# A fused attention and bilinear feed-forward kernel on one core: single-instruction fillers and another order for all engines

## The chip, the cores and the metric

The kernel runs on one core of a Trainium2 chip. A core has five engines with queues of their own, each executing its instructions strictly in the order in which the program gives them: PE (TensorE, the matmuls; its weight loads are shown as PEld), DVE (VectorE), ACT (ScalarE), POOL (GpSimd) and SP (SyncE, which here only issues transfers). POOL and ACT issue a few transfers too. The metric is the device time of one execution in microseconds. Two kernels are told apart by the medians of their runs.

## What is computed

Eight batches of eight heads, 576 positions, head size 64, go through causal attention with a forget gate; the result, as 4608 tokens of 512 values, goes through a bilinear feed-forward layer.

```python
scores = scale * np.matmul(q, k.transpose(0, 1, 3, 2))
log_f = np.log(np.clip(f, 0.0001, 1.0))
cum = np.cumsum(log_f, axis=-1)
decay = cum[:, :, :, None] - cum[:, :, None, :]
scores = np.where(causal, -1000000000.0, scores + decay)
attn = np.exp(scores - max); attn = attn / (sum + 1e-09)
x = (attn @ v), heads side by side: 4608 x 512
out = ((x @ w_a) * (x @ w_b)) @ w_out       # w_a, w_b: 512 x 1536, w_out: 1536 x 512
```

## The kernel before

**Attention.** Work goes by pairs of heads: t = 4b + pair, 32 of them. Half a batch, four heads, is a unit u. For each unit the queries and keys are loaded by SP in fp32 (line 288), cast to fp16 (mostly on POOL), transposed on DVE (line 302), and multiplied on PE in four groups of query blocks (tile sc, line 401). For the first three batches the decay and the causal mask are added on PE with further small matmuls into the same banks; for the others DVE adds a decay row that SP spreads over the partitions (tile spread, line 456), fused with the row maximum (line 512). DVE takes row maxima (line 488), ACT the exponentials with their sums (lines 544 and 550), DVE the reciprocals (lines 557 and 559), POOL scales the probabilities in place (line 567). The probabilities of a pair lie in two tiles: A for the first three query blocks, B for the last two (PA and PB; for four of the first eight pairs the tiles are the spread buffers, spread_78 to spread_81, not yet in use then, and one pair's A tile is an S buffer). They are turned by the DMA (line 583, into PTA and PTB, or for the first two batches partly into spare room of the tile xT) or, for batch 0, by PE (line 591, tile psP). PE multiplies them with the values: lines 611, 613 and 623 (pv) and line 636 (the last 64 rows, pv4). ACT or DVE copies the result, transposed, into xT.

**Feed-forward.** The tokens go in eleven groups: three of 256, then 384, six of 512, and 384. For each of twelve blocks of 128 hidden values PE makes psa and psb, four matmuls each (line 874), ACT or DVE copies psa (tile a, lines 138 and 142), DVE multiplies it with psb into ht (line 890). Then PE multiplies ht with wout into pso (line 899), ACT or DVE copies it into osb, and it is stored (line 914). The weights are loaded and cast by POOL's queue in seven parts (line 365): wa and wb in 512 and 1024 columns, wout in three parts.

**Buffers.** The PSUM has eight banks: two double tiles sc, and four single ones, ff, which psa, psb, pso, pv, psP and the fillers share. A tile is written again once its last readers are done.

**Fillers.** Forty operations multiply the unit matrix by itself into a free ff tile (tile idle, line 178). Nothing reads the result: they only keep PE at work. Each was four matmuls of 128 columns.

**What sets the order.** All the work is first put down as a list of numbered operations (`op`), each with the engines it may go to, its inputs and the buffers it takes. A table, `ORDER`, gives the sequence of these numbers, and `CHOICE` one letter for each operation that may go to more than one engine (A for ACT, D for DVE, P for POOL, S for SP). `laid_out` reads both, and the operations are emitted in that order. So each engine's queue is the table's order, restricted to that engine.

Of the kernel before, what the change touches and what calls it, by code (L numbers as in the profile page):

```python
# [37 lines left out]
def kernel(  # L38
# [11 lines left out]
    nc = tc.nc  # L50
# [29 lines left out]
    ident = fixed("ident", [128, 128])  # L80
# [94 lines left out]
    def filler(_):  # L175
        p = ps.tile([128, 512], FP32, tag="ff", bufs=RING["ff"], name="idle")
        for n in range(4):
            nc.tensor.matmul(out=p[:, 128 * n:128 * n + 128], lhsT=ident, rhs=ident, start=True, stop=True)
# [800 lines left out]
    for t0, n in [(0, 256), (256, 256), (512, 256), (768, 384)] + [(1152 + 512 * n, 512 if n < 6 else 384) for n in range(7)]:  # L979
# [3 lines left out]
        42-44 0 20 41 2 1 64 26 31 23 54 55 45 16 32 13 12 71 46 37 47 56 18 67 27 65 34 72 73 68 48 24 19  # L983
# [3 lines left out]
        142 6 154 155 92 147 143 159 149 91 148 144 160 162 161 108 166-168 145 172 131 52 53 132 179 173 14  # L987
# [13 lines left out]
        1667 1670 455 1671-1673 1676 1677 421 388 382 381 389 456 1674 401 333 1678 357 413 1675 364 1679  # L1001
# [3 lines left out]
        465 460 500 409 463 505 1703 416 1704 480-482 424 508 440 428 422 1705 1706 509 471 477 483 479 510  # L1005
# [5 lines left out]
        1745-1747 1750 1748 548 1749 1752 1751 573 575 543 529 532 618 549 533 1753 1754 577 536 605 537 545  # L1011
        1755 1758 1759 1756 580 582 581 1713 550 552 606 553 1757 554-556 611 583 1760 544 578 585 1762 1763
# [17 lines left out]
        831 874 852 1880 875 1829 883 885 1883 1884 1000 884 841 1882 834 880 1885 911 854 857 886 1888-1890  # L1030
# [105 lines left out]
```

## Time and profile before

| | |
|---|---|
| median of 3 runs | 402.16 us (401.61, 402.16, 402.33) |
| profiled execution | span of 400.7 us from its first to its last instruction; no other time of it is given |
| mean granted TensorE clock | 0.986 |
| busy | PE 96%, DVE 79%, POOL 63%, ACT 62%, PE's weight loads 53% |
| HBM | 49.69 MB read, 9.58 MB written |
| chain that ended last | PE 79%, DMA 9%, DVE 4%, POOL 2%, ACT 2% |

The profile's page tells busy time, then the span in forty slices of 10 us (a digit is tenths of busy time, PEclk the granted clock in tenths), the chain of work that ended last, groups of instructions by line with what ended the idle time before them, and DMA issues with their time to landing. The windows give the same by chosen stretches, the waits say who waited for whom, and the timeline gives single instructions, merged where they follow each other. A row of the timeline is: start in us, length in us, engine, line, operation, output<-inputs, shapes, and in brackets the idle time before it and what ended that. Of an engine's queue (SPq, POOLq) the rows tell the issuing of a transfer, not the transfer.

### The profile page before, as it was taken

The numbers are of one execution on the slowest core, as the hardware profiler recorded it, in microseconds if no ns is written. First come the engines' busy times: TensorE is split into PE (matmuls) and PEld (weight loads), VectorE is DVE, ScalarE is ACT, GpSimd is POOL, SyncE is SP. The second block draws the span as 40 slices with busy tenths as digits, with TensorE's granted clock in tenths as the row PEclk, the third lists the DMA queues.
The fourth block names the chain that finished last, engine by engine and source line by source line (L and its number), as shares of the span: only waits on it lengthen the run. The fifth ranks groups of instructions, "written<-read, shape, count | busy, mean of one in ns | idle before, by whom it ended". The sixth has DMA issues, their size and how long they took to land.

```text
span 400.7 us, 11076 instructions
## 1 busy us (share of the span) xinstructions
PE 383.2 (96%) x4040; PEld 212.0 (53%) x4040; DVE 315.3 (79%) x907; ACT 250.0 (62%) x757; POOL 253.6 (63%) x424
## 2 busy tenths in 40 slices
PE   8598799998999999999999999999999999999996
PEld 7466576765855544454445454544444444444553
DVE  8989798976778988997988889898969892373560
ACT  5798766666667778758785777577868673300011
POOL 3889876887397876897896849787968553000000
PEclk9889999998999999999999999999999999999999
DMA  7999989989999999999999999999997729000102
GB/s 282 240 186 289 204 177 224 213 150 215 208 301 208 227 171 330 201 277 212 295 187 286 211 255 273 233 241 190 276 187 218 157 66 202 28 2 36 71 0 79
DMA packets 148311, 78.22 MB, mean 195 GB/s; under 512 B 130592, under 2 KB 133408, under 8 KB 148256
## 3 DMA queue, kind: packets, MB, share of 16 engines
q1 hardware_dynamic: 144272, 72.53, 77.4%
q0 software_dynamic: 3696, 4.72, 7.0%
q8 instruction: 31, 0.51, 0.5%
q10 hardware_dynamic: 288, 0.26, 0.2%
q14 instruction: 24, 0.20, 0.1%
HBM read 49.69 MB, written 9.58 MB: 148 GB/s over the span
## 4 chain that ended last, share of the span: by engine, by line
PE 79%; DMA 9%; DVE 4%; POOL 2%; ACT 2%; issue 2%; SPq 0%; POOLq 0%; DVEq 0%; ACTq 0%
PE pso L899 22%; PE psa L874 22%; PE psb L874 21%; PE sc L401 8%; DMA wa<-in_moe_w_a_dram 5%; PE pv L611 2%; DVE st L488 2%; DMA k<-in_k_dram 1%; PE pv L613 1%; PE sc L636 1%; DMA PTB<-spread 1%; DMA PTB<-PB 1%; DVE qT L302 1%; PE pv L623 1%; ACT PB L550 1%
## 5 line engine op out<-in xcount | busy, mean ns | idle before, releaser
L874 PE MATMUL psa<-xT,wa 128*128 128x512 f16 (+2 forms) x528 | 116.2, 343 | 2.3 <-DMA wa<-in_moe_w_a_dram 1.7
L874 PE MATMUL psb<-xT,wb 128*128 128x512 f16 (+2 forms) x528 | 116.2, 343 | 0.1
L899 PE MATMUL pso<-wout,ht 128*128 128x512 f16 (+1 forms) x444 | 98.4, 374 | 0.0
L567 POOL TENSOR_SCALAR PA<-PA,st 128x128 f16<-128x128 f16 (+2 forms) x162 | 76.0, 482 | 31.8 <-DVE st L559 20.4
L890 DVE TENSOR_TENSOR ht<-psb,a 128x512 f16<-128x512 f32 (+2 forms) x132 | 76.2, 589 | 22.0 <-PE psb L874 15.0
L512 DVE CUSTOM_DVE_ANT_0 S<-sc,spread 128x128 f32<-128x128 f32 (+3 forms) x160 | 86.7, 567 | 7.7 <-PE sc L401 5.4
L138 ACT CAST a<-psa 128x512 f16<-128x512 f32 (+2 forms) x85 | 43.5, 515 | 55.9 <-PE psa L874 53.8
L874 PEld LDWEIGHTS <-wa 128*128 128x128 f16 x528 | 50.1, 99 | 45.5 <-issue 3.7
L874 PEld LDWEIGHTS <-wb 128*128 128x128 f16 x528 | 50.4, 99 | 41.5 <-issue 1.7
L567 POOL TENSOR_SCALAR PB<-PB,st 128x512 f16<-128x512 f16 (+1 forms) x84 | 58.7, 712 | 15.7 <-DVE st L559 14.6
L550 ACT ACTIVATE PA<-S,st 128x256 f16<-128x256 f32 (+2 forms) x120 | 59.9, 502 | 12.5 <-DVE st L512 12.4
L899 PEld LDWEIGHTS <-ht 128*128 128x128 f16 x444 | 41.7, 98 | 46.8 <-issue 1.3
L488 DVE TENSOR_REDUCE st<-sc 128x2 f32<-128x512 f32 (+7 forms) x68 | 46.3, 723 | 6.0 <-PE sc L401 5.3
L401 PE MATMUL sc<-kT,qT 32*128 32x128 f16 (+5 forms) x960 | 41.7, 272 | 5.5 <-ACT PA L550 2.1
L550 ACT ACTIVATE PB<-S,st 128x512 f16<-128x512 f32 x40 | 28.5, 714 | 7.9 <-DVE st L512 7.9
L401 PEld LDWEIGHTS <-qT 32*128 32x128 f16 (+1 forms) x960 | 18.6, 96 | 26.7 <-issue 14.4
L142 DVE CAST a<-psa 128x512 f16<-128x512 f32 (+2 forms) x47 | 26.2, 560 | 7.2 <-PE psa L874 6.6
L559 DVE RECIPROCAL st<-st 128x2 f32<-128x2 f32 x128 | 18.5, 157 | 14.0 <-ACT PA L550 8.7
L142 POOL CAST k<-k 128x1152 f16<-128x1152 f32 (+1 forms) x15 | 20.5, 1367 | 8.9 <-DMA k<-in_k_dram 8.9
L138 ACT COPY osb<-pso 128x512 f32<-128x512 f32 (+1 forms) x22 | 12.4, 570 | 19.9 <-PE pso L899 15.1
L138 ACT CAST xT<-pv 128x512 f16<-128x512 f32 (+2 forms) x39 | 17.0, 446 | 11.8 <-PE pv L636 5.8
L140 POOL TENSOR_SCALAR q<-q 128x1152 f16<-128x1152 f32 (+1 forms) x15 | 20.6, 1372 | 5.0 <-DMA q<-in_q_dram 4.2
(98 smaller groups left out, 491.5 us busy)
## 6 DMA issues: line engine op xcount, KB each, us to landing
spread<-cum_d SPq DMA_DIRECT2D x20, 576.0 KB, 5.9
out_dram<-osb SPq DMA_DIRECT2D x35, 256.0 KB, 3.8
q<-in_q_dram SPq DMA_DIRECT2D x15, 576.0 KB, 7.3
k<-in_k_dram SPq DMA_DIRECT2D x15, 576.0 KB, 5.2
v<-in_v_dram SPq DMA_DIRECT2D x32, 256.0 KB, 6.1
wout<-in_moe_w_out_dram POOLq DMA_DIRECT2D x3, 512.0 KB, 8.7
v<-in_v_dram SPq DMA_DIRECT2D x8, 128.0 KB, 7.2
wb<-in_moe_w_b_dram POOLq DMA_DIRECT2D x1, 1024.0 KB, 13.5
```

The lines of the kernel that those rows point to most:

```text
L138: nc.scalar.copy(out=out_, in_=in_)
L140: ENG[e].tensor_scalar(out=out_, in0=in_, scalar1=0.125, scalar2=1.0, op0=MUL, op1=MUL)
L142: ENG[e].tensor_copy(out=out_, in_=in_)
L401: nc.tensor.matmul(out=dst, lhsT=lhsT, rhs=rhs, start=start, stop=stop, skip_group_check=True)
L488: nc.vector.tensor_reduce(out=m if i == 4 else st[:, 2 * i:2 * i + 2][:, h:h + 1] if isinstance(x, list) else m, in_=y, axis=AXX, op=MAX, ...
L512: nc.vector.tensor_tensor_reduce(out=o, in0=x, in1=y, scale=-1.0, scalar=3e38, op0=ADD, op1=MIN, accum_out=m)
L550: nc.scalar.activation(out=p_blocks(t, i)[:, :, h, :], in_=x.rearrange("p (j k) -> p j k", k=128), func=EXP, scale=sign, bias=st[:, c:c + ...
L559: nc.vector.reciprocal(out=st[:, 20 + 2 * i:22 + 2 * i], in_=st[:, 10 + 2 * i:12 + 2 * i])
L567: ENG[e].tensor_scalar(out=p, in0=p, scalar1=st[:, c:c + 1], scalar2=1.0, op0=MUL, op1=MUL)
L874: nc.tensor.matmul(out=o, lhsT=w16[:, db, 128 * fb:128 * fb + 128], rhs=tokens(db, t0, n), start=(db == 0), stop=(db == 3))
L890: nc.vector.tensor_tensor(out=ht[:, 0:n], in0=T.pop(("psb", t0, fb))[:, 0:n], in1=T.pop(("a16", t0, fb))[:, 0:n], op=MUL)
L899: nc.tensor.matmul(out=o, lhsT=T[("ht", t0, fb)][:, 128 * tb:128 * tb + 128], rhs=wout16[:, fb, c], start=(fb == 0), stop=(fb == 11))
```

## The change

The operations, their numbers and the buffers are the same. Two things are changed. A filler is now one matmul of 512 columns, the unit matrix read four times over, in place of four of 128. And `ORDER` and `CHOICE` hold another order for all engines and another choice of engines, found by a search which counted that two readers of one PSUM bank wait for each other.

```diff
     def filler(_):
         p = ps.tile([128, 512], FP32, tag="ff", bufs=RING["ff"], name="idle")
-        for n in range(4):
-            nc.tensor.matmul(out=p[:, 128 * n:128 * n + 128], lhsT=ident, rhs=ident, start=True, stop=True)
+        nc.tensor.matmul(out=p.rearrange("p (n k) -> p n k", n=4), lhsT=ident,
+                         rhs=ident.unsqueeze(1).to_broadcast([128, 4, 128]), start=True, stop=True)
...
     CHOICE = """
-        DPAADDAAPPAPAAPADPADDAAADAADDDDDAADDDDAAADAAADDAAAADAAAAADAAAAAAADAAAAAADDAAADADADDAAAAAADDAAAAAAAAA
...
+        APDDAPAAPAPPAAPPDPDDDAADDADDDDAAADDADDAADAAAAADAAAADDAADDADADDAAADAAAAAAADAAAAAAAAAAAADDAADDAAADAAAAA
...
```

PE's queue has 8082 rows before and 7842 now: the 240 that are gone are three matmuls and three weight loads of each filler. Eleven fillers, not sixteen, now stand ahead of PE's first other matmul, and 29, not 24, behind it. The other counts hardly move: DVE copies 48 of the 132 psa tiles (47 before), ACT 84 (85), and the copies of pso, pv and psP are shared out nearly as before.

**POOL, the loads of the weights.** The rows are those of POOL's queue in the first third of batch 0 and 1. Line 365 issues a part of the weights, line 567 scales probabilities, line 142 casts k or v, line 140 q. Before:

```order
L142 CAST nv_73<-v_355 128x1024
L567 TENSOR_SCALAR PA<-PA,st 128x128 x2
L567 TENSOR_SCALAR PA<-PA,st 128x2x128 x2
L365 DMA wa_70<-in_moe_w_a_dram 128x4x512
L567 TENSOR_SCALAR PA<-PA,st 128x2x128 x2
L365 DMA wb_71<-in_moe_w_b_dram 128x4x512
L567 TENSOR_SCALAR PA<-PA,st 128x128
L142 CAST nv_74<-v_377 128x1024
L567 TENSOR_SCALAR spread_80<-spread_80,st 128x2x128
L365 DMA wb_71<-in_moe_w_b_dram 128x4x1024
L365 DMA wa_70<-in_moe_w_a_dram 128x4x1024
```

Now the first part of wb comes ahead of the cast of the next q:

```order
L140 TENSOR_SCALAR q_270<-wout_72 128x640
L365 DMA wb_71<-in_moe_w_b_dram 128x4x512
L140 TENSOR_SCALAR q_276<-q_214 128x1152
L567 TENSOR_SCALAR PA<-PA,st 128x2x128
L567 TENSOR_SCALAR PA<-PA,st 128x128
```

then both parts of wa follow, behind the first norms of spread_79:

```order
L567 TENSOR_SCALAR spread_79<-spread_79,st 128x2x128
L567 TENSOR_SCALAR spread_79<-spread_79,st 128x128
L567 TENSOR_SCALAR spread_79<-spread_79,st 128x2x128
L365 DMA wa_70<-in_moe_w_a_dram 128x4x512
L365 DMA wa_70<-in_moe_w_a_dram 128x4x1024
```

and the large part of wb follows thirteen rows later, with the first part of wout right behind:

```order
L567 TENSOR_SCALAR spread_80<-spread_80,st 128x3x128 x2
L142 CAST k_678<-k_676 128x1152
L567 TENSOR_SCALAR PB_76<-PB_76,st 128x4x128 x2
L365 DMA wb_71<-in_moe_w_b_dram 128x4x1024
L365 DMA wout_72<-in_moe_w_out_dram 128x4x512
```

So the small wb part moved to the front, and the large one from ahead of the large wa part to the end.

**SP, the transposes of batch 1.** Line 583 turns a tile of probabilities, line 272 loads v, line 288 q or k, line 914 stores. Before:

```order
L583 DMA_TRANSPOSE PTB<-PB_76 128x13x128
L583 DMA_TRANSPOSE xT_67<-S 128x6x128
L583 DMA_TRANSPOSE xT_66<-PA 128x6x128
L272 DMA v_1988<-in_v_dram 64x8x64
L583 DMA_TRANSPOSE xT_69<-spread_78 128x6x128 x2
L272 DMA v_2066<-in_v_dram 128x8x64 x2
L583 DMA_TRANSPOSE xT_68<-spread_81 128x6x128 x2
L914 DMA out_dram<-osb 128x512
L583 DMA_TRANSPOSE PTB<-spread_78 128x13x128
L583 DMA_TRANSPOSE PTB<-spread_81 128x13x128
```

Now:

```order
L583 DMA_TRANSPOSE PTB<-PB_77 128x13x128
L583 DMA_TRANSPOSE xT_69<-spread_78 128x6x128
L583 DMA_TRANSPOSE xT_67<-S 128x6x128
L914 DMA out_dram<-osb 128x512
L288 DMA q_1961<-in_q_dram 128x1152
L272 DMA v_2009<-in_v_dram 128x8x64 x2
L583 DMA_TRANSPOSE xT_68<-spread_81 128x6x128
L583 DMA_TRANSPOSE PTB<-spread_78 128x13x128
L583 DMA_TRANSPOSE xT_69<-spread_78 128x6x128
L583 DMA_TRANSPOSE PTB<-spread_81 128x13x128
L583 DMA_TRANSPOSE xT_68<-spread_81 128x6x128
```

Between the second PTB<-PB and PTB<-spread_78 stood ten transfers, now seven: the second halves of both xT transposes moved behind the PTB that follows them, and the store moved ahead.

**PE, the last rows of two pairs of batch 1.** Where PE's scores of one group end, before:

```order
L401 LDWEIGHTS xT0_66
L401 MATMUL sc0_1844<-neg_62,xT0_66 128x2x32
L636 LDWEIGHTS nv1_74
L636 MATMUL pv4_1900<-PTB_1742,nv1_74 64x64
L636 LDWEIGHTS nv1_74
```

Now the same scores are followed by

```order
L401 LDWEIGHTS xT0_66
L401 MATMUL sc0_1735<-neg_62,xT0_66 128x2x32
L874 LDWEIGHTS wa16_70
L874 MATMUL psa_1788<-xT0_66,wa16_70 128x256
L874 LDWEIGHTS wa16_70
L874 MATMUL psa_1788<-xT1_67,wa16_70 128x256
```

and the first product with a tile turned from PB stands behind the last of eight such groups:

```order
L874 MATMUL psb_1863<-xT3_69,wb16_71 128x256
L623 LDWEIGHTS nv1_74
L623 MATMUL pv_1870<-xT0_66,nv1_74 64x128
L623 LDWEIGHTS nv1_74
L623 MATMUL pv_1870<-xT0_66,nv1_74 64x128
L623 LDWEIGHTS nv1_74
L623 MATMUL pv_1870<-PTB_1801,nv1_74 64x128
```

So eight groups of psa and psb, four matmuls each, moved from behind these products to ahead of them. From the 384-token group on, PE's order of scores, products and feed-forward groups is nearly the same in both.

More of the change, by code (lines that the diff above doesn't have):

```diff
@@ L1085 @@
-        2307 2299 2300 2304 2305 2308-2310
+        42 0 14 30 19 43 23 27 20 34 25 13 1 64 44-46 54 55 17 47 56 66 2 48-50 57 71-73 67 36 31 58 61 59
+        51 68 69 32 74 10 75 76 275 21 77 9 70 78 62 79 37 96 80 90 16 60 276 109 115 65 110 111 81-83 117
+        97 112 116 103 11 12 18 114 7 118 120 121 134 122 98 99 104 113 105 128 130 84 106 140 277 146 119
+        124 123 125 85 126 129 131 132 230 127 3 89 141 135 142 91 136 153 155 154 231 143 145 108 100 101
+        278 279 147-149 39 6 137 139 159 160 162 161 166 168 167 172 179 52 180 181 5 138 173 174 156 40 144
@@ new lines @@
+        258 259 102 107 216 217 133 244 169 170 24 41 224 266 245 171 53 252 253 238 175 198 176 225 239 267
+        182 199 200 203 1598 1599 1602 1604 1600 1601 1603 1606 1605 204 272 273 1608 150 274 178 163 177
+        220 92 205 201 207 208 221 4 94 209 212 213 185-187 192 188 184 86 290 291 297 194 193 189 151 152
[3 rows of a table added]
+        366 1625 214 284 243 261 240 241 197 373 374 190 95 1626-1628 191 367 1630-1632 296 1633 215 350 351
+        1629 1634 1636 1635 1638 344 352 375 376 306 1637 378 449 450 300 368-370 372 288 289 262 263 285
[9 rows of a table added]
@@ new lines @@
+        427 623 1650 465 480-482 383 603 385 422 404 405 508 384 510 417 473 499-501 483 506 507 1704 509
[4 rows of a table added]
+        1736 547 549 542 1735 1737 1738 1740 604 1739 1742 1744 1743 569-571 573 463 576 1741 527 1745 575
[4 rows of a table added]
+        1779 591-593 626 671 672 678 1780 638 1770 640 1781 639 645 1784 595 594 1782 606 1783 1786 641 612
+        613 1785 1788 609 642 644 643 1789 1792 596 673 1790 1791 647 674 1793 1794 646 1795-1797 1800 648
+        649 679 681 610 680 624 1798 682 683 597 627 630 607 599 1802 631 634 1787 709 632 633 635 1799 675
@@ new lines @@
+        676 651 614 615 652 653 655 685 801 686 1801 1804 1806 802 1803 1805 1808 1807 1771 1766 684 654 656
+        636 659 1810 677 660 621 1809 688 687 689 691 1811 798 692 693 1812 1814 1813 616 1816-1818 1820 658
[4 rows of a table added]
+        767 777 820 821 778 779 744 1843-1846 745-747 718 719 726 780 748-750 782 783 781 1847 816 817 1848
+        1849 1851 1852 741 727 804 711 1853 1824 1833 784 715 1850 1854 754 755 806 751 809 822 756 796 818
+        752 753 787 788 1855 1856 757 758 760 759 1859 1857 1858 785 786 1861 1860 1862 1863 824 789-792 869
@@ new lines @@
+        877 871 870 1865 876 793 805 794 1864 872 836 1866-1868 843 1869 1870 838 879 873 875 1871 1872 1875
+        1873 1874 906 844 810 1876 846 837 839 807 1877-1879 1881 795 826 825 828 845 811 797 829 847 910
+        832 912 814 907 812 878 830 831 1834 815 880 882 833 850 852 881 851 1880 853 1883 1884 883-886 848
+        999 834 840 842 874 841 849 908 1882 1885 1886 887 888 890 1888 891 1889 1890 854 855 996 856-858
+        892 808 819 859 860 835 862 864 863 893 823 895 896 1893-1895 1898 889 1887 865 1829 866 861 897 914
@@ new lines @@
+        898 899 902 1896 827 911 904 926 933 928 867 959 961 960 1899 1900 1903 1904 934 936 966 962 1891
+        868 903 901 968 900 967 894 997 1905 1907 1906 813 905 998 927 1014 1909 935 1908 1911 1912 1000 937
+        1910 939 963 965 938 915 1001 969-972 1018 929 1913 930 931 1015 1914 918 919 922 920 921 923 973
+        1007 974 964 975 932 976 940 942 941 1892 977 978 1016 1915-1918 943 944 946 1919 1921 1901 924 980
+        947 945 979 948 909 981 913 1019 1920 1922 1923 1925 1924 1926 949 916 917 1004 925 952 953 1020 950
@@ new lines @@
+        1220 1395 1153 1186 1154 2010 2006 1213 1185 1217 1265 1187 1266 1149 1273 2013 2015-2017 1155 1190
+        2014 2019 2020 2018 2021 1232 1234 1240 2024 1156 1192 2025 1267 1268 1275 1182 1191 1188 1233 1189
+        1206 1207 2022 2026 1203 1204 1218 1396 1193 1272 1269 1271 1270 1239 1221 1235-1238 1242 1225 1228
+        1274 1276-1278 1241 1243-1245 1226 2027 1224 1229 1246 1247 1249 1222 1223 1392 1393 1248 1279 1280
+        1282 2029 2030 1250 1230 1286 1287 1302 1303 1281 1251 2031 2034 1306 1308 2028 1283 1285 1284 2032
@@ new lines @@
+        1210 1219 1208 1288 1253-1255 1215 2035 2036 1227 1289 2023 1231 1291 1292 1307 1293 1290 2039 2041
+        1300 2033 1294 1258 1260 1259 2037 2040 2043-2045 1252 1298 1295 1297 1310 1322 1329 1261 1262 2046
+        2047 2049 1296 1324 1263 1256 1257 1264 1330 2048 2051 1211 2050 1331 2053 2052 2055 1209 1323 1325
+        1355 1363 1357 1356 2042 1397 1362 1326 1328 1332 1333 1335 1358 1359 1361 1394 2056-2058 1365 2059
+        2061 1364 2060 1327 2062 2063 1301 1315 1299 1311 1314 1312 1334 1318 1319 1403 1316 1317 2054 1336
@@ new lines @@
+        1337 1339 1338 1404 1369-1371 2064 2067 1360 1366 1304 1367 2065 2066 1320 1408 1410 1368 1340 1341
[3 rows of a table added]
+        1400 1398 1353 2092 2093 1464 2094 2097 2098 1354 1390 1431-1434 2090 1380 1388 1387 1386 1389 1438
+        1399 1416 1391 1437 1419 1471 1423 1440 1473 1472 1439 1474 1476 1424 1475 1422 1435 1426 1401 1441
+        1442 1405 1443 1466 1467 1469 1406 1407 1436 2091 1425 1427 1477-1479 2099 2102 1420 2095 2096 1444
+        1446 1445 1447 1480 1402 1468 1428 1451 1452 1413 1500 1448 1450 2103 2104 1481-1483 1421 2107 2108
@@ new lines @@
+        1449 2109 1484-1486 2105 1429 2110 1456 1457 1453 1458 2111 1454 2113 2112 2115 1487 1417 1489 1490
+        2116 1459 1460 1492 2117 2118 2100 1504 1501 1491 1493 1505 1508 1520 1528 1521 1498 1522 2119-2121
+        2114 1496 2123 1553 1560 1523 1561 1455 2125 2124 1555 1462 1461 1497 1488 1527 1562 1495 1494 2127
+        2128 1554 1556 1499 2122 1557 1558 1563 2126 2129 1409 2131 1564 1529 1530 2132 1531 2133-2135 1509
[4 rows of a table added]
+        2157 2160-2162 2165 1577 2166 2163 2167 2168 2170 2171 1552 1587 1589 1583-1585 1590 1578 1593 1595
@@ new lines @@
+        1596 2172 2175 2176 2169 2177 2173 2174 2178-2180 2183 2181 2182 2158 2184 2187 2185 2186 2188 2191
+        2189 2190 2192 2195 2196 2193 2194 1588 1591 2159 1594 1597 2197-2199 2201 2200 2203 2205 2204 2207
+        2209 2206 2208 2210 2202 2211 2213 2212 2215 2217 2216 2218 2164 2219 2221 2220 2223 2222 2214 2224
+        2225 2228-2231 2226 2233-2235 2238-2240 2243 2244 2227 2236 2245-2248 2232 2249-2251 2241 2252 2255
+        2242 2253 2254 2256 2259 2257 2258 2260 2263-2266 2261 2262 2267 2269 2268 2271 2273 2270 2272 2275
@@ L1091 @@
+        DAADAAADAADAAADADADDADAADAADDADDDADDADDAADDADADAADDAAAAAADAAAADAAADAADAAAAADADDADAADAAAADAAAAADADAAD
+        AADAAAAAAAADAAAAAADAAAAAAAADAADDADDAAAAADAAADADDDDADADDAAADDAAADADDAAADADADSAS
     """
```

46 lines of the change are left out of this document (8 added, 38 removed), and 107 rows, old and new, of the table ORDER.

## The prediction

> **What bounds the kernel now.** I read the page's busy shares first, then the windows (every engine by stretch of time), then PE's waits, then PE's timeline around the two longest late ones.
>
> ```profile
> PE 383.2 (96%) x4040; PEld 212.0 (53%) x4040; DVE 315.3 (79%) x907; ACT 250.0 (62%) x757; POOL 253.6 (63%) x424
> PEclk9889999998999999999999999999999999999999
> ```
>
> PE is busy 96% of a span of 400.7 us. The missing 17.5 us and the low digits of the clock lie early, which the windows show (columns: PE, PEld, DVE, ACT, POOL busy us, clock, DMA share, GB/s).
>
> ```profile
> 10.00:20.00 10.00, 5.28 (x138) 4.01 (x136) 9.62 (x23) 7.67 (x32) 8.86 (x20) 0.86 0.99 240
> 40.00:50.00 10.00, 7.75 (x134) 6.06 (x136) 7.95 (x21) 7.32 (x30) 8.40 (x12) 1.00 1.13 204
> 90.00:100.00 10.00, 8.22 (x100) 5.42 (x100) 6.13 (x13) 6.31 (x18) 7.10 (x13) 0.83 1.07 213
> 120.00:130.00 10.00, 10.00 (x84) 5.89 (x82) 8.30 (x30) 7.85 (x27) 7.88 (x10) 1.00 1.09 207
> 380.00:390.00 10.00, 10.00 (x62) 5.95 (x61) 6.93 (x13) 1.44 (x3) 0.00 (x0) 1.00 0.00 0
> ```
>
> From 120 to 390 us PE has no hole and full clock, and its arithmetic is the same after the change. So the time can only be won or lost ahead of some 110 us, and in the last 5. PE's own waits, over the span:
>
> ```profile
> PE sc L401 <- ACT PA L550: 2.1, 1, 2.1
> PE sc L401 <- DVE st L559: 2.1, 1, 2.1
> PE pv L636 <- DMA PTB<-spread: 1.8, 1, 1.8
> PE psa L874 <- DMA wa<-in_moe_w_a_dram: 1.7, 1, 1.7
> PE pv L636 <- DVE st L488: 0.8, 1, 0.8
> ```
>
> The first two lie at 13 to 18 us, while VectorE is busy 9.62 of 10: there PE waits for the softmax and is not the bound. After that PE is behind with its work only because of three things: the second part of wa, and two transposed probability tiles. Their places:
>
> ```profile
> 44.21 0.61 PE L874 MATMUL psa<-xT,wa 128*128 128x256 f16 x4 [1.65 <-DMA wa<-in_moe_w_a_dram]
> 78.27 0.35 PE L636 MATMUL pv<-PTB,nv 128*64 128x64 f16 x10
> 79.45 0.35 PE L636 MATMUL pv<-PTB,nv 128*64 128x64 f16 x10 [0.84 <-DVE st L488]
> 94.28 0.35 PE L636 MATMUL pv<-PTB,nv 128*64 128x64 f16 x10 [1.77 <-DMA PTB<-spread]
> 95.58 0.93 PE L874 MATMUL psa<-xT,wa 128*128 128x256 f16 x4
> 98.86 0.73 PE L874 MATMUL psa<-xT,wa 128*128 128x256 f16 x4
> 101.36 0.61 PE L874 MATMUL psa<-xT,wa 128*128 128x256 f16 x4
> 101.80 0.60 PE L874 MATMUL psb<-xT,wb 128*128 128x256 f16 x4
> PEld L636 <- DMA PTB<-PB: 1.2, 2, 0.9
> ```
>
> The wait of 0.84 is put down to a reduction, but the weight loads of the same line sat 0.9 for the DMA PTB<-PB, whose transpose is the younger of two; I take the DMA. Behind the wait of 1.77, four groups (psa, psb, psa, psb) take 98.86 - 95.58 = 3.28 us, where one takes 101.80 - 101.36 = 0.44 at full clock: 3.28 - 4 x 0.44 = 1.5 us lost to the low clock in the slice 90 to 100.
>
> **The change part by part. Fillers.** Forty fillers stand in each version. One was four instructions, now it is one of the same width.
>
> ```profile
> 9.48 0.84 PE L178 MATMUL idle<-ident 128*128 128x128 f16 x12
> 11.52 0.62 PE L178 MATMUL idle<-ident 128*128 128x128 f16 x8
> 160.18 1.04 PE L874 MATMUL psa<-xT,wa 128*128 128x512 f16 x4
> 161.06 1.03 PE L874 MATMUL psb<-xT,wb 128*128 128x512 f16 x4
> ```
>
> Four narrow ones cost 0.84 - 0.62 = 0.22 us; one 512 wide costs (161.06 - 160.18) / 4 = 0.22. Seven of them stand behind the wa wait in both orders. I take 0; the ends are -0.5 (a quarter of the instructions, all forty cheaper by 0.013) and +0.5 (the clock rises later, since eleven now stand ahead of the first other matmul instead of sixteen).
>
> **Weights.** They are loaded from POOL's queue, and the order of the four parts changes.
>
> ```profile
> 17.05 0.98 POOL L365 DMA_DIRECT2D wa<-in_moe_w_a_dram  x1
> 21.71 0.81 POOL L365 DMA_DIRECT2D wb<-in_moe_w_b_dram  x1
> 22.51 0.75 POOL L365 DMA_DIRECT2D wa<-in_moe_w_a_dram  x1
> 30.44 1.39 POOL L142 CAST k<-k 128x1152 f16<-128x1152 f32 x1
> wb<-in_moe_w_b_dram POOLq DMA_DIRECT2D x1, 1024.0 KB, 13.5
> wa<-in_moe_w_a_dram POOLq DMA_DIRECT2D x1, 1024.0 KB, 21.7
> ```
>
> Before, both 1024 KB parts were issued by 22.5; they landed at 21.71 + 13.5 = 35.2 and 22.51 + 21.7 = 44.2, so the last megabyte took 9 us behind the other. Now the 512 KB of wb go out first, ahead of a cast of q, but the large wb part goes out last, behind the cast of k and two norms of PB. That cast ended at 30.44 + 1.39 = 31.8 before; the changed order has 47 POOL rows ahead of the large wb part, the old one 44 up to the end of that cast, of like kinds, so I put the issue at 32.2. The large wa part is queued behind the first norms of spread_79 in both orders, so near 22.5 as before; with the large wb part no longer ahead of it, it is in well before 44, and PE's wait moves from psa to the psb behind it, which before started 0.44 later, at 44.7. With 13.5 the part lands at 45.7, with 9 us behind wa at about 45; I take +0.7. What is queued behind PE's wait is the whole score group of the next pair, and VectorE behind that, as before. The ends are -1.7 (no wait) and +9.2 (21.7 from 32.2); the range of the likely case goes to +1.9.
>
> **The two late tiles.** At 78 us PE's order put the two PTB<-PB products right behind the scores; now eight psa and psb groups (8 x 0.44 = 3.5 us) stand between. The wait of 0.8 goes: -0.8, with 0 as the other end if POOL's norms of PB come that much later. For PTB<-spread the SP queue matters.
>
> ```profile
> 83.66 0.75 POOL L567 TENSOR_SCALAR spread<-spread,st 128x576 f16<-128x576 f16 x1
> 84.96 4.37 SPq L583 DMA_TRANSPOSE xT<-spread  x2
> 89.37 0.58 SPq L914 DMA_DIRECT2D out_dram<-osb  x1
> 90.06 3.54 SPq L583 DMA_TRANSPOSE PTB<-spread  x2
> PTB<-spread SPq DMA_TRANSPOSE x2, 4.3
> ```
>
> The last norm of spread_78 ended at 84.4, yet its transpose was issued at 90.06: SP was still busy with two other transposes and a store. Now seven transfers instead of ten stand between the second PTB<-PB and this transpose, and only one of the two transposes of spread_81. The q and v loads ahead of it wait for casts that POOL does ahead of that norm, so they don't hold it. Its issue falls between 84.5 and 87, it lands 4.3 later, at 88.8 to 91.3, and PE asks at 92.5 - 0.8 = 91.7. The wait goes: -1.8. The low clock came with that hole; with the hole filled I take -1.5.
>
> [...]
>
> **What is late next.** PE then comes 4.1 us sooner to the products of the next pair:
>
> ```profile
> 97.24 1.36 POOL L567 TENSOR_SCALAR PB<-PB,st 128x512 f16<-128x512 f16 x2 [1.75 <-DVE st L559]
> 96.54 0.42 DVE L142 CAST a<-psa 128x256 f16<-128x256 f32 x1 [1.54 <-PE psa L874]
> 100.75 4.57 SPq L583 DMA_TRANSPOSE PTB<-PB  x2
> 108.18 0.51 PE L636 MATMUL sc<-PTB,nv 128*64 128x64 f16 x20
> ```
>
> Those transposes were only just in time (105.3 is the end of the second issue, 108.18 the use). But their norms stood behind a VectorE copy that itself waited 1.54 us for the stalled psa, so most of the chain moves up with PE. I take +0.7; ends 0 and +4.1 (the chain does not move at all). In the last 5 us the two stores move from ScalarE's queue to SP's; a last store has to be issued and to land in either case, so I take 0 for it.
>
> **The sum.** 0 + 0.7 - 0.8 - 1.8 - 1.5 + 0.7 = -2.7 on the span of 400.7, so 398.0. The median of the runs, 402.16, is 1.5 above that span; the profile gives no other time for its execution, so I keep the 1.5 and forecast 399.5. Its own range, with weights from -1.7 to +1.9 and the chain up to +2: 397.1 to 401.5.
>
> **Rivals.** (1) The gain is given back: the norms and transposes of the next pair stay where they are, +4.1 instead of +0.7, against -4.1 won, and 402.2 with the weights hidden, 402.9 with +0.7. For it speaks that the use at 108.18 had little room; against it, that the chain hung on the same stall. (2) The weights end on the other side. The large wb part now leaves some 10 us later than before; if it needs the 21.7 us of the slower row, PE stands from 44.7 to 53.9, +9.2, and the three later losses (4.1) vanish under it: 407.3; with 17.6, the mean of the two rows, +5.1 - 4.1 = +1.0, 403.2. It decides from a landing at 44.7 + 4.1 = 48.8 us. Against it: 21.7 was the second of two megabytes in the queue, and 512 KB of wb are out of the way sooner. I put it at 404.5. (3) The wb part is in time: the sum loses 0.7 and the old wait of 1.7 too, 397.1. [...] (4) The clock falls anyway, because the early stretch leaves PE as thin as before: -1.2 instead of -2.7, 401.0.
>
> **How the numbers follow.** Chances: forecast 0.42, (1) 0.17, (2) 0.25, (3) 0.07, (4) 0.09. Runs of this kernel spread by 0.7 us, so 0.2% (0.8 us) is about what can be told from no change. Faster is the forecast, (3) and (4): 0.58; same is (1): 0.17; slower is (2): 0.25. The range goes from 396.9, a little under (3), to 404.4, which leaves out the worse half of (2), 0.12, and a few hundredths below. The likeliest case alone is 397.1 to 401.5.
>
> **What would show it.** In the changed profile: PE's wait before line 874 near 44 us names wb, not wa, and is 1 to 3 us; no wait of line 636 for PTB<-spread above 0.5; clock 1.00 in the windows from 90 to 110; the first 384-wide group of psa earlier by about 3 us; no hole from 120 on. The forecast is wrong if wb lands past 48.8, if PE waits over 2 us for PTB<-PB near 104, or if a wait appears past 120 us where now there is none.

## The result and the profile after

| | before | after |
|---|---|---|
| median | 402.47 us (16 runs) | 405.92 us (16 runs, 403.05 to 408.87) |
| profiled execution | span 400.7 us | 407.46 us, span 405.7 us |
| mean granted clock, profiled | 0.986 | 0.974 |

The ratio is 1.0086, with a 95% interval of 1.0062 to 1.0109: the change makes the kernel 3.5 us slower. The forecast was 2.7 us faster, and the time lies above the stated range. Slow runs, far above the others of their kernel, are left out of every figure; of the kernels below that is 411.47 us in late_new, 420.58 in late_letters and 967.7 in issue_first.

First the page of the changed kernel, two of its rows, with the same columns as before:

```profile
PE 386.9 (95%) x3920; PEld 205.0 (51%) x3920; DVE 315.2 (78%) x907; ACT 249.2 (61%) x755; POOL 254.1 (63%) x426
PEclk9658999999999999999999999999999999999999
```

The work is the same; PE's 386.9 is 3.7 us more for the same arithmetic, since it runs longer at half clock (between the clock's first rise and 110 us for 20.5 us, before for 10.2). That low clock now lies at the start (6, 5, 8 in the second to fourth slice) and no longer in the slice from 90 us, as the windows show:

```profile
10.00:20.00 10.00, 5.42 (x91) 2.64 (x90) 8.31 (x14) 5.92 (x21) 5.44 (x8) 0.67 1.07 220
20.00:30.00 10.00, 9.14 (x103) 4.69 (x103) 8.81 (x21) 8.67 (x35) 7.93 (x17) 0.50 0.86 171
30.00:40.00 10.00, 9.34 (x161) 6.68 (x160) 8.57 (x24) 6.76 (x19) 8.46 (x12) 0.86 0.97 200
90.00:100.00 10.00, 9.34 (x156) 6.14 (x152) 8.46 (x20) 6.10 (x18) 8.97 (x17) 1.00 1.15 169
```

Now PE's waits (who waited, for whom; us in total, times, longest):

```profile
PE sc L401 <- DVE qT L302: 3.7, 1, 3.7
PE sc L636 <- DMA PTB<-PB: 2.2, 3, 0.8
PE psb L874 <- DMA wb<-in_moe_w_b_dram: 1.0, 1, 1.0
PE pv L623 <- DMA xT<-spread: 0.5, 1, 0.5
PE psa L874 <- DVE ht L890: 0.5, 1, 0.5
```

The two late waits of before are gone, and the wait for wa has become one for wb, as forecast. But a wait of 3.7 us for qT stands at the start, and new ones stand where before had none. They begin behind 120 us, in PE's timeline:

```profile
131.06 0.35 PE L636 MATMUL sc<-PTB,nv 128*64 128x64 f16 x10 [0.65 <-DMA PTB<-PB]
164.78 1.02 PE L874 MATMUL psa<-xT,wa 128*128 128x512 f16 x4 [0.32 <-DVE a L142]
190.96 1.02 PE L874 MATMUL psa<-xT,wa 128*128 128x512 f16 x4 [0.16 <-DVE osb L142]
195.65 0.35 PE L636 MATMUL sc<-PTB,nv 128*64 128x64 f16 x10 [0.80 <-DMA PTB<-PB]
239.27 1.02 PE L874 MATMUL psa<-xT,wa 128*128 128x512 f16 x4 [0.46 <-DVE ht L890]
```

The windows of twenty microseconds from 120 to 340 us and the rest to 395 us, summed, before first and after second:

```profile
sum 275.00, PE 274.95 PEld 132.57 DVE 214.70 ACT 165.94 POOL 164.56; mean PE 22.91 PEld 11.05 DVE 17.89 ACT 13.83 POOL 13.71
sum 275.00, PE 271.70 PEld 129.96 DVE 211.65 ACT 166.20 POOL 165.03; mean PE 22.64 PEld 10.83 DVE 17.64 ACT 13.85 POOL 13.75
```

Before, PE was busy 274.95 of 275; now it stands 3.3 us, and that counts only the gaps that the modelled ends of the matmuls leave open.

To see where the time goes I read three places of PE's order from each trace: the start of the first matmul of psa, of the 321st matmul of line 874 (its first three token groups and eight blocks of the fourth are then done), and of the last one, the 1056th. Whatever the order, the same matmuls of that line lie between them.

| | first psa | from it to the 321st | from there to the last |
|---|---|---|---|
| before | 30.4 | 95.2 | 263.7 |
| after | 34.2 | 91.2 | 268.9 |
| difference | +3.8 | -4.0 | +5.2 |

So the middle won 4.0 us in this pair of executions, near what was forecast, and both ends lost. Behind the last psb nothing changed: 400.7 - 389.24 = 11.5 and 405.7 - 394.33 = 11.4.

### The profile page after: what moved, and what is told of

The parts are those of the page before. It is cut to its first block, busy times and chain, and to the rows that moved or that the text cites. A ratio compares the mean times of both kernels' runs of the same rounds, so it can differ in the third digit from the quotient of the medians.

```text
span 405.7 us, 10810 instructions
## 1 busy us (share of the span) xinstructions
PE 386.9 (95%) x3920; PEld 205.0 (51%) x3920; DVE 315.2 (78%) x907; ACT 249.2 (61%) x755; POOL 254.1 (63%) x426
## 4 chain that ended last, share of the span: by engine, by line
PE 57%; DMA 12%; DVE 11%; POOL 9%; issue 5%; ACT 4%; SPq 1%; POOLq 0%; DVEq 0%; ACTq 0%
PE psb L874 17%; PE psa L874 16%; PE pso L899 12%; PE sc L401 6%; DVE S L512 5%; DMA spread<-cum_d 4%; DMA wb<-in_moe_w_b_dram 3%; POOL PA L567 3%; DMA PTB<-PB 3%; POOL PB L567 2%; ACT PB L550 2%; POOL spread L567 2%; PE pv L611 2%; DVE qT L302 1%; DVE st L488 1%
## 5 line engine op out<-in xcount | busy, mean ns | idle before, releaser
L567 POOL TENSOR_SCALAR PA<-PA,st 128x256 f16<-128x256 f16 (+2 forms) x162 | 75.1, 478 | 38.7 <-DVE st L559 33.3
L401 PE MATMUL sc<-kT,qT 32*128 32x128 f16 (+5 forms) x960 | 42.6, 276 | 6.0 <-DVE qT L302 3.7
L138 ACT COPY osb<-pso 128x512 f32<-128x512 f32 (+1 forms) x24 | 13.6, 571 | 24.1 <-PE pso L899 16.6
L567 POOL TENSOR_SCALAR spread<-spread,st 128x256 f16<-128x256 f16 (+4 forms) x36 | 19.6, 552 | 11.7 <-DVE st L559 9.1
L550 ACT ACTIVATE PA<-sc,st 128x256 f16<-128x256 f32 (+2 forms) x42 | 19.4, 481 | 9.1 <-DVE st L488 7.9
```

The source lines that it names most:

```text
L138: nc.scalar.copy(out=out_, in_=in_)
L401: nc.tensor.matmul(out=dst, lhsT=lhsT, rhs=rhs, start=start, stop=stop, skip_group_check=True)
L550: nc.scalar.activation(out=p_blocks(t, i)[:, :, h, :], in_=x.rearrange("p (j k) -> p j k", k=128), func=EXP, scale=sign, bias=st[:, c:c + ...
L567: ENG[e].tensor_scalar(out=p, in0=p, scalar1=st[:, c:c + 1], scalar2=1.0, op0=MUL, op1=MUL)
```

## Experiments

**What was asked.** My theory after the result: the changed order costs time in the first 35 us and, by small stops, behind 120 us, and wins in the middle. The rivals: that the late stops only follow from an early delay; that they come from the engines chosen; that the fillers lower the clock. Since the operations are the same, a valid order can be put together from parts of both tables: the first N operations of one, then the rest in the order of the other. The table gives all runs; ratio and interval are against runs of before on the same chip, the three stages are those above, from one profiled execution each. The runs come from three chips, on which before's median was 401.68 to 402.76, so rows are best compared by their ratios.

| run | median | ratio (95%) | mean clock | first psa | to 321st | to last |
|---|---|---|---|---|---|---|
| before, again | 400.48 (one run) | | 0.991 | 30.1 | 93.1 | 264.1 |
| after, again | 406.12 (one run) | | 0.979 | 31.8 | 93.6 | 267.6 |
| late_old | 405.52 | 1.0084 (1.0052-1.0116) | 0.978 | 30.1 | 95.2 | 266.1 |
| late_new | 407.02 | 1.0101 (1.0046-1.0155) | 0.985 | 30.3 | 92.8 | 270.8 |
| early_old | 403.92 | 1.0049 (1.0013-1.0085) | 0.986 | 30.4 | 89.9 | 268.9 |
| mid_new183 | 404.67 | 1.0069 (1.0030-1.0108) | 0.983 | 32.8 | 93.2 | 269.2 |
| ends_old | 402.27 | 1.0017 (0.9988-1.0047) | 0.985 | 30.4 | 93.1 | 263.7 |
| wb_later | 405.32 | 1.0085 (1.0051-1.0120) | 0.983 | 29.8 | 92.4 | 267.6 |
| late_letters | 415.32 | 1.0343 (1.0280-1.0406) | 0.981 | 30.6 | 94.3 | 275.9 |
| fill1 | 401.63 | 1.0000 (0.9972-1.0028) | 0.988 | 30.3 | 93.4 | 265.1 |
| late_front | 403.86 | 1.0041 (1.0000-1.0082) | 0.985 | 31.5 | 93.3 | 266.3 |
| issue_beside | 400.82 | 0.9964 (0.9923-1.0005) | 0.987 | 30.8 | 91.8 | 264.4 |
| issue_beside2 | 400.23 | 0.9969 (0.9940-0.9999) | 0.988 | 32.7 | 92.4 | 264.3 |
| issue_first | 400.54 | 0.9981 (0.9947-1.0014) | 0.988 | 30.8 | 91.2 | 265.8 |

The mean clock of the runs of before lay at 0.986 to 0.987 in these comparisons; that of the 16 runs of the change was 0.980.

### Early, middle, late: orders joined

```diff
-ORDER = after
+late_old:   after[:770],                     then the rest as in before
+late_new:   before[:772],                    then the rest as in after
+early_old:  before[:183],                    then the rest as in after
+mid_new183: before[:183], then after[:770],  then the rest as in before
+ends_old:   before[:183], then after[:718],  then the rest as in before
```

The letters of `CHOICE` go with each part. Fillers are those of after, in late_new and mid_new183 those of before.

> The changed order up to the row that PE reaches at 120 us, then the order and the engine choices of before; fillers single. Theory (the late part of the changed order itself stops PE: 5.2 us between 120 and 345 us in the profile of the change, none of it in that of before): about 402, that is 0.0 to -1.0 against before, and no wait of PE after 120 us above 0.2. Rival (the late stops follow from how far the other engines are behind at 120 us, so they come with the early part): 405 to 406.5, with waits for PTB<-PB or for the copies of a after 120 us.

> The order of before up to the row that PE reaches at 120 us, then the changed order and engine choices; fillers of four instructions. Theory (the late part itself stops PE): 405 to 407.5, +3 to +5 against before, with PE waits after 120 us that sum to 2 to 4 us. Rival (the stops come with the early part): within 0.5 of before.

> The order of before for the first 183 operations (to the row that PE reaches at about 30 us), then the changed order; fillers single. Theory (the first 35 us of the changed order cost 3.9 us: the cast of q on VectorE takes 2.5 instead of 1.2, PE stands 3.7 us, the clock stays at half until 32.8): 401 to 403, 3 to 4 below the change, and the clock at full from about 24 us. Rival (what PE loses early it gets back from the waits in the middle, where transfers would be late anyway): 405 to 406.5, with longer waits for wb, PTB and xT between 45 and 110 us.

> The first 183 operations and everything from 120 us on in the order of before; only the stretch between in the changed order; fillers of four instructions. Theory (the middle stretch is what the change wins, about 3.9 us, and both ends lose): 398 to 399.5. Rival (the middle wins only because PE comes to it late, after a slow start): 401.5 to 403, with the waits for wb, PTB<-PB and PTB<-spread back.

Three of these four told less than meant, because the join itself stops PE. In mid_new183 a mask on POOL waited for its load at the join, VectorE for the mask, ScalarE for VectorE, and PE 3.57 us for ScalarE:

```profile
128.90 0.42 DVE L512 CUSTOM_DVE_ANT_1 S<-sc,spread 128x256 f32<-128x256 f32 x1 [4.30 <-POOL spread L462]
130.39 1.44 PE L874 MATMUL psb<-xT,wb 128*128 128x384 f16 x4 [3.57 <-ACT a L138]
```

late_old has 1.2 us of the same kind; late_new a wait of 2.0 us for PTB<-PB at its join. Taken alone, late_old's 405.52 lies in its rival's range, late_new's 407.02 in its theory's, and mid_new183's 404.67 in neither; with these waits at the joins they decide nothing. early_old is clean: with the early part of before the first psa is at 30.4, as in before, and the median is 2.0 us below the change's (I expected 3 to 4), 1.5 by the ratios, whose intervals overlap. Its late part still takes 268.9 us. PE's waits behind 120 us there:

```profile
PE sc L636 <- DMA PTB<-PB: 1.8, 2, 1.0
PE psa L874 <- DVE ht L890: 0.5, 1, 0.5
PE psa L874 <- DVE a L142: 0.3, 1, 0.3
PE psb L874 <- DVE a L142: 0.3, 1, 0.3
```

These are the change's own late stops, though PE came there 5.1 us sooner. The early delay is not their cause. The join was then put elsewhere:

> The first 183 operations in the order of before, then the changed order to the row that PE reaches at 107 us, then the order and engine choices of before; fillers single. The join lies at another place than in the run with both ends old, where a mask on POOL that waited for its load held VectorE for 4.3 us at the join. Theory (the middle wins 3 to 5 us and the changed late order loses 5 of them in small stops): 398.5 to 400.5, no PE wait above 0.3 after 120 us. Rival (what is won before 107 us is lost afterwards whatever the order): 402 to 404.

No seam is seen in this one; all that is left of PE's waits behind 120 us is one row:

```profile
PE sc L636 <- DMA PTB<-PB: 0.2, 1, 0.2
```

The late part takes 263.7 us, as in before. The order of before there, then, is worth 5.2 us against early_old's execution, with the same order ahead of the join; the medians, 402.27 and 403.92, give 1.7, the ratios 1.3, again with intervals that overlap. But the median was expected at 398.5 to 400.5, and lies in the rival's range of 402 to 404. Its late part gives nothing back, so the rival's reason does not hold either: the middle of the changed order wins less than I read off the first profile (below).

### Is it chance?

> The kernel before, profiled a second time. Theory (the half clock at 95 us in the first profile belongs to that execution and not to the order): full clock from about 24 us to the end, wait for PTB<-spread between 1 and 2 us, PE at the products of the next pair 1.5 to 3 us sooner than in the first profile, the late part without a stop of over 0.2 on psa or psb. Rival (the low clock follows from the order's hole): half clock for one window between 92 and 100 us again.

> The changed kernel, profiled a second time. Theory (the stops behind 120 us are in the order): the same first matmuls stop for the same time within 0.05 us (0.49, 0.33, 0.24, 0.31, 0.63, 0.23, 0.42), and PE loses 3.9 to 5.3 us there; before 120 us the time differs from the first profile by up to 5 us, with the number of half-clock windows. Rival (they come from what the transfers do in one execution): other places, other sizes.

Both kernels as they are. The stops on psa and psb behind 120 us come back at the same matmuls with the same size: the differences of start to start, less the matmul's own time, are 0.49, 0.24, 0.31, 0.63, 0.26, 0.23 and 0.42 us in both profiles of the change (the first has two more, of 0.33 and 0.18; I had expected the 0.33 again). Six of the seven, all but the 0.26, stand in early_old and wb_later too, within 0.01. In seven executions with the late order of before behind 120 us (before twice, fill1, ends_old, the three with the moved issue) no stop of psa or psb exceeds 0.15. They are in the order.

The waits for PTB<-PB are not: behind 120 us they come to 0.9 to 1.8 us in the four undisturbed executions of the changed late order (after twice, early_old, wb_later), but to 0 to 1.7 in those seven, of which fill1 has the most, and issue_first has one stop of 1.7 on sc that is put down to ht:

```profile
PE sc L636 <- DMA PTB<-PB: 1.7, 2, 1.4
PE sc L636 <- DVE ht L890: 1.7, 1, 1.7
```

The whole late part took 267.6 to 268.9 in those four, and 263.7 to 265.8 in the seven: means 268.3 and 264.4, 3.8 us apart. The stops on psa and psb sum to 2.5 to 3.1 us in the four, so they are most of it.

The middle is the opposite. In the second execution of before the clock stays at full from 90 to 100 us, and the wait for PTB<-spread is 1.0, not 1.8; in the second of the change the same window is at 0.83, behind a wait that before does not have. Rows: the window and the wait of before, then window and timeline of the change, each in its second execution:

```profile
90.00:100.00 10.00, 8.53 (x181) 6.41 (x179) 6.90 (x15) 6.54 (x21) 8.72 (x15) 1.00 1.10 219
PE pv L636 <- DMA PTB<-spread: 1.0, 1, 1.0
```

```profile
90.00:100.00 10.00, 7.58 (x91) 5.13 (x90) 5.77 (x13) 4.89 (x16) 6.55 (x12) 0.83 1.11 186
95.13 0.29 PE L623 MATMUL pv<-xT,nv 128*64 128x128 f16 x2 [2.42 <-DMA xT<-spread]
```

From first psa to the 321st before took 95.2 and then 93.1, the change 91.2 and then 93.6. Over four executions of before's order there (95.2, 93.1, 93.4, 92.8) the mean is 93.6; over nine of the changed one 92.9 (a join lies shortly before the end of some). The middle wins 0.7, not 4.0; with 92.8 to 95.2 in the one set and 89.9 to 95.2 in the other, 0.7 cannot be told from nothing.

### The late stops

> The changed order, with the engines of the copies behind the row of 120 us as before chose them (61 copies go to the other one of ScalarE and VectorE). Theory A (the late stops come from which engine copies): PE's waits after 120 us fall under 1 us, the median to 401 to 403. Theory B (they come from the place of the copies and products in VectorE's queue, behind transposes of k and sums that wait): the waits stay at 2 us or grow, 405.5 to 408.

```diff
-CHOICE = after
+CHOICE = after, but for copies behind 120 us as in before (61 letters)
```

It got 9.4 us slower than the change, far above both expectations. Letters and order belong together, so this decides nothing on what makes the stops; theory B's waits did grow, to a late part of 275.9 us. The next run asks VectorE directly. In the change's first profile VectorE does this ahead of PE's stop at 239.27:

```profile
236.24 0.69 DVE L142 CAST a<-psa 128x512 f16<-128x512 f32 x1 [0.69 <-PE psa L874]
237.41 0.17 DVE L559 RECIPROCAL st<-st 128x2 f32<-128x2 f32 x1 [0.48 <-ACT PA L550]
237.49 1.21 DVE L302 STREAM_TRANSPOSE kT<-k 128x576 f32<-128x576 f32 x1
238.54 1.87 DVE L890 TENSOR_TENSOR ht<-psb,a 128x512 f16<-128x512 f32 x3
```

A reciprocal waits for ScalarE's sum, a transpose of k follows, and the product whose psb has long been done, and whose bank PE wants, starts at 238.54.

> The changed order behind the first 183 operations of before, as in the run with the early part old, with four instructions of VectorE moved ahead in its queue behind 120 us: a product ahead of a sum's reciprocal and the transpose of k (the place of the 0.63 us stop), a copy of pso and two copies of psa ahead of pieces of the decay step (the places of the 0.33, 0.48 and 0.42 us stops). Nothing moves on PE, POOL or SP. Theory (each stop is a reader that stands in VectorE's queue behind other work): those four stops vanish, the others keep their hundredths, PE loses 3.3 to 3.8 instead of 5.2 us behind 120 us; the median 402 to 403.5 against 403.9. Rival (VectorE has too much work there, so another stop of the like size takes each place): the loss stays at 5 us, 403.5 to 405.

VectorE's queue at one of the four places; the other three move a copy in the same way:

```diff
 L142 CAST a_4743<-psa 128x512
+L890 TENSOR_TENSOR ht<-psb,a_4712 128x512
 L559 RECIPROCAL st<-st 128x2
 L302 STREAM_TRANSPOSE kT<-k_4748 128x9x64
-L890 TENSOR_TENSOR ht<-psb,a_4712 128x512
```

The four stops are gone, the 0.24, 0.31 and 0.23 stand unmoved, and against early_old two are new, of 0.20 and 0.22 (the second at the place of the 0.26). PE's waits behind 120 us are one row:

```profile
PE sc L636 <- DMA PTB<-PB: 0.6, 1, 0.6
```

The late part takes 266.3 where early_old's took 268.9: 2.6 less, more than the 1.4 to 1.9 expected, but 1.2 of it is from PTB<-PB (0.6 for 1.8), which differs by 0.6 between the change's own two executions. For these four stops the mechanism is shown: a reader that stands in VectorE's queue behind other work. For the three that stand unmoved it is not tested. The median does not show it: 403.86, in the rival's range and above the expected 402 to 403.5, with a ratio of 1.0041 against 1.0049. A microsecond is within these intervals.

### The fillers

> Before with single fillers, nothing else. Theory (a filler costs the same either way): within 0.5 of before, 401.6 to 402.6, and the same mean clock of 0.986. Rival (single fillers keep the clock lower, which would be the lower clock of the change): 403.5 to 405, mean clock 0.980 to 0.982.

The edit is that of the filler alone. 1.0000, and the clock is not lower (0.988, against 0.986 to 0.987 for before): within the interval of 0.28%, the forty fillers cost the same either way.

### The early part

> The change with one operation moved: the issue of the first part of wb on POOL goes behind the cast of v, some 6 us later. Theory (that issue runs beside VectorE's cast of q and makes it take 2.5 us instead of 1.2): the cast is back at 1.2, PE's wait for qT falls from 3.7 to about 2.4, the median falls by 1.0 to 2.5 to 403.5 to 405. Rival (the cast is slowed by the scaling of q on POOL beside it, not by the issue): the cast stays at 2.3 to 2.5 and the time at 405.5 to 406.5.

```diff
 L140 TENSOR_SCALAR q_270<-wout_72 128x640
-L365 DMA wb_71<-in_moe_w_b_dram 128x4x512
 L140 TENSOR_SCALAR q_276<-q_214 128x1152
 L567 TENSOR_SCALAR PA<-PA,st (three)
 L142 CAST nv_73<-v_287 128x1024
+L365 DMA wb_71<-in_moe_w_b_dram 128x4x512
```

> The kernel before with one operation moved: the issue of the first part of wb goes ahead of POOL's scaling of q, so that it stands beside VectorE's scaling of the other q at 12.6 us. Theory (the issue of a load on POOL slows that VectorE instruction): it takes 2.2 to 2.6 instead of 1.2, PE's second scores come 1.0 to 1.4 us later, and the median is 0.3 to 2 above before. Rival (the slow cast was something else's): 1.2, and within 0.5 of before.

```diff
+L365 DMA wb_71<-in_moe_w_b_dram 128x4x512
 L140 TENSOR_SCALAR q_339<-q_332 128x1152
 L142 CAST nv_73<-v_355 128x1024
...
-L365 DMA wb_71<-in_moe_w_b_dram 128x4x512
```

In wb_later VectorE's cast fell from 2.48 to 0.97 and PE's wait for qT from 3.7 to 2.2, as the theory had it; the median, 405.32, came out above the expected 403.5 to 405. But issue_beside, which puts the issue beside the cast, has the cast at 0.56, not at the expected 2.2 to 2.6. The theory that the issue by itself makes the cast that slow fell. Here are the VectorE row and POOL's rows beside it, of after, of before and of issue_beside:

```profile
13.57 2.48 DVE L140 TENSOR_SCALAR q<-wout 128x512 f16<-128x512 f32 x1
13.33 0.98 POOL L365 DMA_DIRECT2D wb<-in_moe_w_b_dram  x1
14.34 1.41 POOL L140 TENSOR_SCALAR q<-q 128x1152 f16<-128x1152 f32 x1
```

```profile
12.65 1.16 DVE L140 TENSOR_SCALAR q<-wout 128x512 f16<-128x512 f32 x1
12.13 1.40 POOL L140 TENSOR_SCALAR q<-q 128x1152 f16<-128x1152 f32 x1
```

```profile
12.64 0.56 DVE L140 TENSOR_SCALAR q<-wout 128x512 f16<-128x512 f32 x1
11.99 0.98 POOL L365 DMA_DIRECT2D wb<-in_moe_w_b_dram  x1
```

The cast ends at 16.05, 13.81 and 13.20; the POOL instruction that it was beside ends at 15.75, 13.53 and 12.97. The gap is 0.30, 0.28, 0.23, and 0.28, 0.29 and 0.23 in wb_later, issue_beside2 and issue_first. So in these six a cast that came behind a POOL instruction, be it a scaling or an issue, ended 0.23 to 0.30 us after that one's end. In the first execution of the change the next POOL instruction began 0.03 us after the first and took 1.41, and the cast ended only behind that one. The change's second execution, with the same order, does not have this:

```profile
13.06 0.43 DVE L140 TENSOR_SCALAR q<-wout 128x512 f16<-128x512 f32 x1
13.12 1.09 POOL L140 TENSOR_SCALAR q<-wout 128x640 f16<-128x640 f32 x1 [2.35 <-DVE st L488]
```

In seven of the sixteen executions the cast came no later than POOL's instruction, or within 0.01 us of it, and took 0.42 to 0.43. In five of these the POOL instruction was the scaling of 1152 columns, which took 1.56 to 1.71 instead of 1.40. So the 2.48 belong to one execution and not to the order: late_old and late_letters, which begin like the change, have 0.46 and 0.42. That the cast was shorter in wb_later says nothing of the moved issue.

So the two went slower side by side: the cast ended by those gaps behind POOL's instruction, and in those five executions POOL's scaling took 0.16 to 0.31 us more than 1.40. By what means the one holds up the other no trace here shows.

By the ratios, 1.0085 against 1.0086, wb_later gained nothing. The cast is not needed for PE's early wait either: in the change's second execution it took 0.43, and PE still waited 2.8 us for qT. What differs more is the clock. Behind its first rise and ahead of 35 us it stood at half for 20.5 and 13.7 us in the change's two executions and for 13.7 in late_old and late_letters; in the eight executions that begin like before it did so for 6.8 to 13.7, 9.8 in the mean. In wb_later's execution it was 6.8, but its runs have a mean clock of only 0.983. Which of the early moves thins PE out there was not found.

issue_beside itself came out faster than before, and was run again, as it is and with single fillers:

> Before with only the first issue of wb moved ahead of POOL's scaling of q, the same kernel as the run of that name, over five rounds. Theory (the parts of the weights leave POOL about 0.5 us sooner, the last part of wa lands before PE asks for it, and VectorE's cast of q is not held behind POOL): no wait of PE for wa or wb, cast at 0.5 to 0.6, ratio 0.994 to 0.998. Rival (the first result was chance): ratio 0.999 to 1.002.

> The same with single fillers. Theory (fillers cost the same either way): within 0.3% of the run without them and under before, ratio 0.993 to 0.998. Rival (fewer instructions ahead of the first scores keep the clock lower): ratio 0.999 or more, mean clock under 0.984.

0.9964, 0.9969 (upper end 0.9999) and 0.9981: about 1.2 us faster than before, the only version here that beats both kernels, though just outside or inside what these intervals tell from no change. None of its three executions has a wait for wa or wb; with before's early order the wait for wa was 1.7, 1.8, 1.1 and 0.7 in four profiles (before twice, fill1, late_new). The cast was not always at 0.56: in issue_beside2 it lost to POOL's next scaling and took 1.46. So the gain goes with the wait for the weights, not with the cast; more than that they go together is not shown. The rival of a lower clock with single fillers fell (0.988).

## Why the prediction was wrong

- **Fillers, 0.** Right: 1.0000, give or take 0.28%.
- **Weights, +0.7.** Right in kind: the large wb part left POOL at 35.26 (I put it at 32.2) and landed 12.1 later, and PE waited 1.0 for it, with psb named. Against the 1.7 for wa that is -0.6, inside the bounds but the other way from the +0.7.
- **PTB<-PB at 78 us, -0.8, and PTB<-spread, -1.8.** Both waits are gone from the change's profiles, though late_letters, whose order is the change's, has 2.3 us for PTB<-spread. But the second has a successor: the transposes of xT<-spread now stand between the two of PTB<-spread on SP, and PE waited 0.5 or less for xT<-spread in three executions with the changed middle and 2 us or more in six. I named the wait for PTB<-PB at 108 us as the one that would be late next (+0.7, and it was 0.70 in the first profile); the one that mattered came before it.
- **Half clock, -1.5.** Wrong, because the loss belonged to one execution. It is in one of seven executions with before's order there, and around 95 us in three of nine with the changed one (in a fourth at 85.5). With the 0.8 by which the wait for PTB<-spread was shorter in before's second execution, that is 2.3 of the 3.3 between 4.0 won and 0.7.
- **From 120 to 390 us nothing can change.** This is the step that failed most. That PE had no hole there was true of the old order; it said nothing of how close VectorE's and ScalarE's readers came to PE's needs. I compared PE's order, found it nearly the same, and did not compare VectorE's. Measured: +3.8 on the means, 5.2 in the first profile, most of it in stops of 0.2 to 0.6 us on psa and psb that come back at the same matmuls; four of them vanished when their readers were moved ahead in VectorE's queue.
- **The first 30 us.** I gave them the fillers' half microsecond and nothing else. The means of the first psa, 31.7 for four starts in the changed order (34.2, 31.8, 30.1, 30.6) and 30.8 for eight of before's, differ by 0.9, all of it from the execution at 34.2. Executions with as low a clock as that one are common among the runs: five of the change's 16 have its clock of 0.974 or 0.975, while none of the 91 runs of before whose clock is listed is under 0.978. The mean clock of the change is 0.980, that of early_old 0.986 and that of ends_old 0.985, near before's, and early_old is 2.0 us faster than the change.
- **The tail, 0, and the +1.5 between span and time.** The tail is right. The profiled runs show 407.46 - 405.7 = 1.8 for the change and 400.48 - 398.7 = 1.8 for before, so the first profile of before was near 402.5, an ordinary run though its middle was not.
- **Rivals.** (2), at 404.5, is nearest in time and wrong in cause: wb landed at 35.26 + 12.1 = 47.4, short of the 48.8 from which it decides. (1) and (4) are half seen: the middle's gain was given back, at xT<-spread and by the clock. None spoke of VectorE's queue.
- **The likeliest range.** Its upper end does not come out of its terms: with the weights at +1.9 and the chain at +2 the sum is 399.5 + 1.2 + 1.3 = 402.0, not 401.5. The measured 405.92 is above either.

Two accounts of the 3.5 us, then. By the ratios: early 1.0086 - 1.0049 = 0.37% (1.5 us), late 1.0049 - 1.0017 = 0.32% (1.3), and the middle 0.17% the wrong way (0.7). The intervals of neighbouring ratios overlap, so no single step is told from nothing by them; that wb_later stands beside the change (1.0085, 1.0086) and late_front beside early_old (1.0041, 1.0049) speaks for the early one. By the means of the stages in the traces: +0.9, +3.8 and -0.7. Both have the two ends losing and the middle winning next to nothing; on the size of the late part they differ, and why is open, since a trace is one execution and the other runs have none. Also open is what in the early order makes its loss: half clock and PE's wait for qT go with it, the long cast does not.

## What to carry to other kernels

A bound engine without holes is no proof that its stage is safe from a new order: compare the queues of the engines that free its buffers, and look for a reader that stands behind a wait or a long instruction. Before a gain is read off a bad spot of one profile, see whether the spot comes back in a second profile of the same kernel. And when a wait is removed by moving a transfer ahead in a queue, the transfer that it passed is the next suspect.

## What the runs showed of the hardware

- **The clock's windows start at another place in each execution.** The clock changes at multiples of 3.41 us from each other, and it first rises between 4.0 and 7.0 us in the 16 traces. Where a hole lies in these windows then counts as well as its length. In late_front a hole of 2.10 us lay in one window, and the next ran at half clock; in wb_later a boundary cut a hole of 2.74 in two, and the clock stayed full. The holes and the windows of 3.41 us, first of late_front, then of wb_later:

```profile
94.63 0.31 PE L623 MATMUL pv<-xT,nv 128*64 128x128 f16 x2 [2.10 <-DMA xT<-spread]
91.26:94.67 3.41, 1.09 (x42) 0.67 (x36) 1.65 (x3) 0.49 (x2) 3.41 (x6) 1.00 1.01 144
94.67:98.09 3.42, 3.42 (x27) 2.50 (x28) 1.51 (x3) 1.72 (x5) 0.04 (x1) 0.50 1.11 218
```

```profile
93.55 0.25 PE L623 MATMUL pv<-xT,nv 128*64 128x128 f16 x2 [2.74 <-DMA xT<-spread]
88.78:92.20 3.42, 2.03 (x47) 1.01 (x45) 2.66 (x6) 1.13 (x5) 3.42 (x7) 1.00 1.26 157
92.20:95.61 3.41, 2.06 (x29) 1.81 (x30) 0.90 (x2) 1.44 (x4) 1.07 (x2) 1.00 0.87 179
95.61:99.02 3.41, 3.41 (x96) 2.87 (x94) 2.68 (x9) 2.36 (x8) 2.34 (x4) 1.00 1.13 193
```

  Cut into such windows from each trace's first rise, the 16 traces show, between 31 and 390 us, seven falls, behind windows with PE busy for 12, 29, 32, 43, 44, 44 and 48% of the time. Behind all others the clock stayed full, the least busy being 44, 48, 49 and 49%. Ahead of 31 us it also fell behind busier ones, up to 76%, so PE's busy share is not the whole measure.

  The mean clocks of runs lie in steps of 0.004, which is one window (1.7 us of lost full clock in 402), and the change's time follows them: 408.0 us is the mean of its five runs at 0.974 and 0.975, 406.8 of three at 0.979, 404.7 of six at 0.982 and 0.983; of the last two, one at 0.987 took 403.2, but one at 0.990 took 405.5.
- **A stop that comes from the order is as exact as a clock.** Seven stops kept their size within 0.01 us over two executions that differed by 2.4 us at the first psa, and six of them over four.
- **VectorE's cast of 0.42 us took 2.48 in one execution**, behind two POOL instructions that followed each other 0.03 us apart.
- **A reader of scores waited for another.** In before's profile a row maximum on VectorE, at 61.23 us, stood 0.63 us until an exponential on ScalarE that reads sc too had ended; in the change's one at 65.42 stood 1.19. The traces name the tile, not its bank.
